# Four steps of the opening moved by one to seven slots: hash of batch 1's first pair, a turn and the load of its second pair, the last value sums of batch 0

## The chip, the cores and the metric

The kernel runs on one core of a Trainium2 chip. The metric is the device time of one launch in microseconds; lower is better. The names of the engines in the profile: PE is TensorE (PEld is its weight load), DVE is VectorE, ACT is ScalarE, POOL is GpSimd, and SP only issues transfers.

## The reference

Attention in which a query sees only keys with the same hash, followed by a gated feed-forward layer over the result. B = 4 batches, H = 8 heads, S = 768 positions, D = 64.

```python
q_bits = (einsum('bhsd,dk->bhsk', q, proj) > 0)          # 6 bits; k_bits likewise
mask = q_bucket[:, :, :, None] == k_bucket[:, :, None, :]
scores = where(mask, scale * q @ k.T, -1e9)
attn = exp(scores - max) ; attn = attn / (sum(attn) + 1e-9)
x = (attn @ v) as 3072 rows of 512
xn = x / sqrt(mean(x * x) + 1e-6) * rms_g
g = xn @ w_gate ; val = xn @ w_val                         # 512 -> 1536
out = (g * sigmoid(g) * val) @ w_out                       # 1536 -> 512
```

All inputs and the output are float32; the kernel multiplies in float16 except for the hash and the turns of q and k.

## The kernel before

**Units and slots.** The work is cut into eight units u, two per batch b, each with half of the batch's 768 queries. For a head of a unit there are three chunks of scores of 256 keys by 384 queries. One chunk is one slot, so there are 8 x 24 slots. Slot t of the main loop (lines 888 to 894) issues `scores` for chunk t + 1 (two matmuls, L349), `probs` for chunk t (one exponential on ACT, L361), and then what the list `plan[t]` holds for the slot, in the order in which it was put there by `at`. The order on every engine and queue is the order of the program: an instruction that waits holds back all that stands behind it on its engine. In its first 16 heads the order goes over the two units of batch 0. The pair-wise numbering (b, hp) means heads 2 hp and 2 hp + 1 of batch b.

**What a pair needs before its scores.** For the four pairs of batch 0 and the first two of batch 1:
- the load: `load_natural` for k and q and `load_v` for v, three transfers of 384 KB on SP's queue (L97, L106), into a ring of eight buffers, tag "L";
- four turns, `turn_pe`: three TensorE transposes each (L156) into a PSUM bank and a copy on DVE to kT or qT (L158);
- casts to float16 in the tile QK (L178, on POOL or DVE);
- the hash, `hash_pair`: sixteen float32 matmuls into two PSUM banks (L238), and two DVE operations that turn their signs into bits (L227);
- `send_pair`: four small transfers on SP's queue (L277) of 6 rows of bits each into rows 64 to 69 of QK, in the order k and q of the first head, k and q of the second. Scores take these six rows along as additional rows of the product, so equal hashes raise the score.

**Sums of the values.** `v_mean` adds the values of a pair over all positions with matmuls against a tile of ones (L333) and scales the result into cvb (L336), a small constant that stands for the 1e-9 in the reference. Batch 0's first pair takes it from one matmul, the other three from six. `attn_out` (L388 to L401) adds cvb to the product of probabilities and values, divides, and squares for the norm; that of the fourth pair runs in slot 31.

**Banks.** All of turns, hashes, sums, gates and projections take their PSUM bank from one ring of three (tag "g", line 60); a step waits until the bank that it takes was read by its last user. Scores have a ring of two of their own, and the products with the values (`av`, L374, two parts per head, in the slots 1 and 2 above a multiple of three) one bank.

**Around the change.** Slots 8 to 17 turn and hash the last pairs of batch 0. Slots 22 to 32 turn and hash the first two pairs of batch 1, whose scores start in slot 47. POOL issues the loads of the gate and value weights in slots 22, 25 and 31 (L585). Slot 31 ends the attention of unit 0; its norm and its transposition follow until slot 37, with a few idle matmuls (L580) in slots 34 to 36. From slot 38 on the matmuls of the feed-forward layer (L484, L513) are spread over the slots.

The times of the steps stand in two tuples. For a pair of batch 1 the second holds: load; four turns (k of both heads, q of both heads; the first is also when the pair's buffers are taken); cast of k; cast of q; hash; send; the value's cast and sums. The hash and the send of the second pair do not go by the tuple but are placed in slots 32 and 38.

Of the kernel before, what the change touches and what calls it, by code (L numbers as in the profile page):

```python
# [33 lines left out]
def kernel(  # L34
# [563 lines left out]
    def at(w, s, f, *a):  # L598
        plan[NS * w + s].append(lambda: f(*a))
# [75 lines left out]
    at(0, 6, v_prep, 0, 1)  # L675
    at(0, 15, v_prep, 0, 2)
    at(0, 19, v_prep, 0, 3, nc.vector)
    for hp, t in enumerate((6, 16, 21, 28)):
        at(0, t, v_mean, 0, hp, 2, *([range(6)] if hp else []))
    for i, (t, t2) in enumerate(((22, 25), (31, 31))):  # L680
        cols = slice(i * DFF // 2, (i + 1) * DFF // 2)
# [2 lines left out]
        at(0, 39 + 3 * i, load_w, wo, moe_w_out, 6 * i, 6)  # L684


    for hp, ts in ((0, (8, 22, 23, 24, 25, 24, 39, 26, 28, 42)), (1, (20, 27, 28, 29, 30, 29, 41, 32, 33, 43))):
        tl, ts = ts[0], ts[1:]
        for w in "kq":
            at(0, tl, load_natural, nc.sync, 1, hp, w)  # L690
        at(0, tl, load_v, nc.sync, 1, hp)
        at(0, ts[0], new_pair, 1, hp)
        for t, hh, w in zip(ts[0:4], (0, 1, 0, 1), "kkqq"):
            at(0, t, turn_pe, 1, hp, hh, w)
        at(0, ts[4], cast_pool, 1, hp, "k")
        at(0, ts[5], cast_pool, 1, hp, "q")
        if hp == 0:
            at(0, ts[6], hash_pair, 1, hp)
            at(0, ts[7], send_pair, 1, hp)
        at(0, ts[8], v_prep, 1, hp)  # L700
        at(0, ts[8], v_sum, 1, hp)
# [33 lines left out]
    for n, (u, h) in enumerate(order):  # L735
        t = 3 * n + 4 - ((u, h) == (0, H - 1))
# [128 lines left out]
    def behind_norm(t):  # L865

        return t - t % NS + 9 if 1 <= t % NS < 9 else t

    for (b, hp), (load, kturns, qturns, _) in spots.items():
# [3 lines left out]
        for w, turns in (("k", kturns), ("q", qturns)):  # L873
            for i, t in enumerate(turns):
                at(0, t, turn_dve, b, hp, w, i, len(turns))
            t = turns[-1] + 1
            at(0, t if (b, hp) == (1, 2) else behind_norm(t), cast_pool, b, hp, w)
        t = 54 if (b, hp) == (1, 2) else behind_norm(qturns[-1] + 2)
# [69 lines left out]
```

## Time and profile before

| | us |
|---|---|
| median of 3 runs (lowest, highest) | 326.93 (326.87, 327.19) |
| the profiled execution | 326.68 |
| its span, first to last instruction | 324.9 |
| PE busy | 319.9 |
| DVE busy | 229.7 |
| ACT busy | 228.4 |
| POOL busy | 157.6 |

The granted clock of TensorE is 0.999 over the span. Rows of the timeline give the start, the length, the engine, the line in the kernel, the operation with its output and inputs, and how often; the bracket at the end is the idle time before and what ended it. Matmuls overlap, so a row's length is longer than the time until the next one starts. Rows of windows give a stretch, its length, the busy time and number of instructions of each engine, the granted clock, the DMA share and the GB/s moved.

### The profile page before, as it was taken

Reading aid. Unit: us, or ns where it says so; the run is one execution under the profiler, and the core shown is the slowest. Engines: PE = TensorE matmul, PEld = TensorE weight load, DVE = VectorE, ACT = ScalarE, POOL = GpSimd, SP = SyncE. Lnnn points to the kernel's source line nnn. Section 1 sums busy time; section 2 is a strip of 40 time slices with the busy share of each in tenths; the row PEclk is TensorE's granted clock in tenths of the full one; section 3 lists DMA queues with packets and bytes.
Section 4 is the critical chain, followed back from the end, with each engine's and each line's share of the span. In section 5 each row is a group of like instructions: output and inputs, shape, how many; then the busy total and the mean of one; then the engine's idle time right before and its main releaser. Section 6 shows DMA issues by size and latency. Waiting matters only on the chain.

```text
span 324.9 us, 7772 instructions
## 1 busy us (share of the span) xinstructions
PE 319.9 (98%) x2955; PEld 194.4 (60%) x2955; DVE 229.7 (71%) x512; ACT 228.4 (70%) x333; POOL 157.6 (49%) x204
## 2 busy tenths in 40 slices
PE   8999999999999999999999999999999999999996
PEld 3676666656566565655566565655666556665554
DVE  5887876859888568874888568785677536673870
ACT  7999887667688676776767776777777768744322
POOL 4999759955974363731883621752582111221000
PEclk9999999999999999999999999999999999999999
DMA  7942999988428864055547056002100030003002
GB/s 208 360 168 85 226 216 195 192 159 151 103 38 158 157 136 88 6 94 156 89 100 145 35 125 120 7 5 66 72 4 3 1 99 34 0 2 105 10 2 97
DMA packets 85741, 32.63 MB, mean 100 GB/s; under 512 B 70908, under 2 KB 82632, under 8 KB 85704
## 3 DMA queue, kind: packets, MB, share of 16 engines
q1 hardware_dynamic: 81800, 27.35, 36.1%
q0 software_dynamic: 3680, 4.72, 8.5%
q8 instruction: 23, 0.38, 0.5%
q14 instruction: 14, 0.11, 0.1%
q10 hardware_dynamic: 224, 0.07, 0.1%
HBM read 28.58 MB, written 6.29 MB: 107 GB/s over the span
## 4 chain that ended last, share of the span: by engine, by line
PE 98%; ACT 1%; DVE 0%; issue 0%
PE s_ps L349 20%; PE g_ps L484 19%; PE v_ps L484 19%; PE y_ps L513 18%; PE o_ps L374 11%; PE d_ps L218 2%; PE t_ps L156 2%; PE d_ps L238 2%; PE z_ps L580 1%; PE x_ps L467 1%; PE y_ps L532 1%; PE m_ps L333 1%; ACT psb L361 1%; DVE kT L158 0%; PE s_ps L156 0%
## 5 line engine op out<-in xcount | busy, mean ns | idle before, releaser
L361 ACT ACTIVATE psb<-s_ps,ebias 128x768 f16<-128x768 f32 x192 | 167.7, 900 | 20.0 <-PE s_ps L349 19.2
L349 PE MATMUL s_ps<-QK 128*128 128x384 f16 (+1 forms) x384 | 93.5, 326 | 1.2 <-ACT psb L361 1.1
L492 ACT ACTIVATE t<-g_ps 128x384 f32<-128x384 f32 x96 | 47.2, 492 | 52.2 <-PE g_ps L484 50.5
L484 PE MATMUL g_ps<-xnT,wg 128*128 128x384 f16 x384 | 82.7, 326 | 0.0
L484 PE MATMUL v_ps<-xnT,wv 128*128 128x384 f16 x384 | 81.8, 326 | 0.0
L501 DVE SCALAR_TENSOR_TENSOR a<-t,g_ps 128x384 f32<-128x384 f32 x96 | 53.0, 552 | 28.9 <-ACT t L492 27.2
L395 POOL TENSOR_TENSOR x<-otmp,rcp 128x384 f32<-128x384 f32 x30 | 25.1, 837 | 96.2 <-DVE rcp L393 95.8
L513 PE MATMUL y_ps<-wo,ht 128*128 128x512 f16 x276 | 67.7, 379 | 0.0
L502 DVE SCALAR_TENSOR_TENSOR ht<-a,v_ps 128x384 f16<-128x384 f32 x96 | 53.2, 554 | 11.5 <-PE v_ps L484 3.6
L374 PEld LDWEIGHTS <-psb 128*128 128x128 f16 x1152 | 51.9, 97 | 15.7 <-issue 1.2
L374 PE MATMUL o_ps<-vl,psb 128*128 128x65 f16 x1152 | 55.8, 193 | 0.0
L349 PEld LDWEIGHTS <-QK 128*128 128x128 f16 (+1 forms) x384 | 34.8, 98 | 33.7 <-issue 7.9
L484 PEld LDWEIGHTS <-wg 128*128 128x128 f16 x384 | 35.2, 97 | 21.2
L484 PEld LDWEIGHTS <-wv 128*128 128x128 f16 x384 | 35.1, 97 | 20.8 <-issue 0.2
L513 PEld LDWEIGHTS <-ht 128*128 128x128 f16 x276 | 24.9, 98 | 23.0
L525 ACT COPY ysb<-y_ps 128x512 f32<-128x512 f32 x23 | 13.5, 587 | 15.8 <-PE y_ps L513 15.8
L388 DVE TENSOR_TENSOR otmp<-o_ps,cvb 128x390 f32<-128x390 f32 x32 | 17.8, 557 | 7.1 <-PE o_ps L374 7.1
L208 POOL CAST QK<-qT 64x768 f16<-64x768 f32 x20 | 16.5, 823 | 10.3 <-DVE qT L195 9.5
L401 POOL TENSOR_TENSOR sq<-x 128x384 f32<-128x384 f32 x24 | 19.9, 828 | 1.9
L208 POOL CAST QK<-kT 64x768 f16<-64x768 f32 x20 | 16.4, 822 | 5.2 <-DVE kT L195 3.1
L473 DVE TENSOR_TENSOR xnT<-x_ps,gcol 128x512 f16<-128x512 f16 x11 | 7.4, 688 | 15.1 <-PE x_ps L467 15.0
L195 DVE STREAM_TRANSPOSE kT<-kL 128x192 f32<-128x192 f32 x32 | 16.4, 516 | 0.0
(85 smaller groups left out, 274.9 us busy)
## 6 DMA issues: line engine op xcount, KB each, us to landing
vn<-in_v_dram SPq DMA_DIRECT2D x16, 384.0 KB
out_dram<-ysb SPq DMA_DIRECT2D x23, 256.0 KB
qL<-in_q_dram SPq DMA_DIRECT2D x40, 96.0 KB
kL<-in_k_dram SPq DMA_DIRECT2D x40, 96.0 KB
kn<-in_k_dram SPq DMA_DIRECT2D x5, 384.0 KB
qn<-in_q_dram SPq DMA_DIRECT2D x5, 384.0 KB
wg<-in_moe_w_gate_dram POOLq DMA_DIRECT2D x2, 768.0 KB, 9.4
wv<-in_moe_w_val_dram POOLq DMA_DIRECT2D x2, 768.0 KB, 11.7
```

The lines of the kernel that those rows point to most:

```text
L208: nc.gpsimd.tensor_copy(QK[b, 2 * hp + hh, "h"][0:64, o : o + S], src[64 * hh : 64 * hh + 64, :])
L349: nc.tensor.matmul(ps[:, j, 0:HALF], QK[b, h, "h"][rows, S + jt * 128 : S + (jt + 1) * 128], QK[b, h, "h"][rows, half * HALF : (half + 1) ...
L361: nc.scalar.activation(psb[u, h][:, 2 * ch : 2 * ch + 2, :], sps.pop((u, i))[:, :, 0:HALF], AF.Exp, bias=ebias, scale=ESCALE,)
L374: nc.tensor.matmul(o[:, c, hh, 0:65], psb[u, h][:, jt, c * 128 : (c + 1) * 128], vls[b % 2][:, h, 2 * (jt % 3) + jt // 3 if b in PARITY el ...
L388: nc.vector.tensor_add(tmp[:, :, :, 0:65], o[:, :, :, 0:65], cvb[b % 2][:, 2 * hp : 2 * hp + 2, 0:65].unsqueeze(1).to_broadcast([128, 3, 2 ...
L395: eng.tensor_mul(xd.rearrange("p c (h d) -> p c h d", h=2), tmp[:, :, :, 0:64], r.to_broadcast([128, 3, 2, 64]),)
L401: eng.tensor_mul(sq, xd, xd)
L484: nc.tensor.matmul(ps, w[:, kt, fs], xnT[u][:, kt, :], start=(kt == 0), stop=(kt == 3))
L492: nc.scalar.activation(t, fbank[u, ft, "g_ps"], AF.Tanh, scale=0.5)
L501: nc.vector.scalar_tensor_tensor(out=a, in0=t, scalar=1.0, in1=g, op0=ALU.add, op1=ALU.mult)
L502: nc.vector.scalar_tensor_tensor(out=ht[u][:, ft, :], in0=a, scalar=0.5, in1=vv, op0=ALU.mult, op1=ALU.mult)
L513: nc.tensor.matmul(y, ht[u][:, ft, c * 128 : (c + 1) * 128], wo[:, ft, :], start=(ft == 0), stop=(ft == NF - 1),)
```

## The change

Four steps are moved to other slots; nothing is added or removed.
- `v_mean` of batch 0's fourth pair goes from slot 28 to slot 21, behind that of the third pair.
- `hash_pair` of (1, 0) goes from slot 26 to slot 27. Its send stays in slot 28.
- The first turn of (1, 1) (k of its first head, with the taking of its buffers) goes from slot 27 to slot 26. The other turns stay.
- The three load transfers of (1, 1) go from slot 20 to slot 17, which on SP's queue is ahead of the four sends of (0, 3) in slot 18.

```diff
-    for hp, t in enumerate((6, 16, 21, 28)):
+    for hp, t in enumerate((6, 16, 21, 21)):
         at(0, t, v_mean, 0, hp, 2, *([range(6)] if hp else []))
...
-    for hp, ts in ((0, (8, 22, 23, 24, 25, 24, 39, 26, 28, 42)), (1, (20, 27, 28, 29, 30, 29, 41, 32, 33, 43))):
+    for hp, ts in ((0, (8, 22, 23, 24, 25, 24, 39, 27, 28, 42)), (1, (17, 26, 28, 29, 30, 29, 41, 32, 33, 43))):
         tl, ts = ts[0], ts[1:]
         for w in "kq":
             at(0, tl, load_natural, nc.sync, 1, hp, w)
         at(0, tl, load_v, nc.sync, 1, hp)
         at(0, ts[0], new_pair, 1, hp)
         for t, hh, w in zip(ts[0:4], (0, 1, 0, 1), "kkqq"):
             at(0, t, turn_pe, 1, hp, hh, w)
```

## The prediction

> **What bounds the kernel now.** I read the page's busy shares and chain first, then the busy time by stage, and then every engine in order of time from 24 to 46 us, where slots 17 to 38 lie. The page:
>
> ```profile
> PE 319.9 (98%) x2955; PEld 194.4 (60%) x2955; DVE 229.7 (71%) x512; ACT 228.4 (70%) x333; POOL 157.6 (49%) x204
> PE 98%; ACT 1%; DVE 0%; issue 0%
> ```
>
> TensorE is the bound over the whole span, and the change removes no matmul. It can only gain where PE stands idle or is held up by something beside it. The busy time by stage (stretch, its length, then PE, PEld, DVE, ACT, POOL, the granted clock, DMA share and GB/s) says where that is:
>
> ```profile
> 25.90:28.43 2.53, 2.11 (x30) 1.51 (x29) 2.04 (x5) 2.53 (x4) 2.34 (x3) 1.00 0.02 7
> 28.43:35.99 7.56, 7.56 (x105) 5.87 (x104) 5.66 (x14) 6.63 (x8) 5.80 (x7) 1.00 0.79 207
> 35.99:44.35 8.36, 8.34 (x120) 5.47 (x118) 7.03 (x21) 8.18 (x13) 4.80 (x6) 1.00 1.21 209
> ```
>
> Slots 19 to 21 (first row): ACT is full, PE idles 0.42 us. Slots 22 to 29 (second row): PE is full, ACT idles 0.93. Slots 30 to 37 (third row): ACT is nearly full, and PE is padded with idle matmuls. PE in order of time:
>
> ```profile
> 26.85 0.48 PE L349 MATMUL s_ps<-QK 70*128 70x384 f16 x2 [0.39 <-ACT psb L361]
> 27.18 0.44 PE L374 MATMUL o_ps<-vl,psb 128*128 128x65 f16 x9
> 27.64 0.48 PE L349 MATMUL s_ps<-QK 70*128 70x384 f16 x2
> 27.97 0.51 PE L333 MATMUL m_ps<-vl,ones 128*128 128x130 f16 x6
> 28.43 0.48 PE L349 MATMUL s_ps<-QK 70*128 70x384 f16 x2
> 28.76 0.49 PE L156 MATMUL t_ps<-ident,kn 128*128 128x128 f32 x3
> ```
>
> The lengths overlap; what an operation costs is the distance to the next start. Scores cost 0.33 (27.64 to 27.97), a turn 0.33, an AV part 0.27 to 0.28, a mean 0.35 (at 23.15 it is followed by AV at 23.50, and at 34.45 by a turn at 34.80). So the mean of slot 21 leaves PE free at 28.32, and the next scores start at 28.43: 0.11 us of slack, the last before PE runs without a gap. The weight loads of the hash in slot 26, and DVE beside them:
>
> ```profile
> 32.30 0.11 PEld L238 LDWEIGHTS d_ps<-kT,pj 64*32 64x32 f32 x2 [0.32 <-issue]
> 32.41 0.14 PEld L238 LDWEIGHTS d_ps<-qT,pj 64*32 64x32 f32 x4
> 33.18 0.33 PEld L374 LDWEIGHTS <-psb 128*128 128x128 f16 x9 [0.62 <-issue]
> 31.15 1.21 DVE L158 COPY qT<-t_ps 128x384 f32<-128x384 f32 x2 [0.37 <-PE t_ps L156]
> ```
>
> The last weights of the hash load at 32.41, just after the DVE copy of the last turn ends (31.15 + 1.21 = 32.36). From the hash's first load to the next operation's it takes 0.88. The hashes of slots 17 and 32, which follow no fresh turn, take 0.80 (24.28 to 25.08, 38.29 to 39.09).
>
> **The change part by part**, on the profiled execution (326.68 us, span 324.9, 1.78 around it).
>
> *Mean of batch 0's fourth pair, slot 28 to 21.* It leaves slot 28, where PE is full: -0.35. In slot 21 it follows the other mean: PE is free at 28.67 instead of 28.32, and the scores that started at 28.43 start at 28.67: +0.24. Its operands are there: DVE wrote that pair's v at 26.18 to 26.73. Its PSUM bank, third in the ring of three, was last read by the signs of slot 17 (over by 26.27). Its DVE scaling (0.27 to 0.29) falls near 28.9, before the turn's copy that starts at 29.29. ACT's chain: its softmax of 29.22 needs scores that now end near 29.20, so it holds; the next two slip by about 0.1 us, which PE does not feel, since it needs each only a slot later.
>
> *Hash of (1,0), 26 to 27; turn of (1,1), 27 to 26.* PE's sum stays, but the hash no longer follows the copy of slot 25 directly: 0.88 becomes 0.80, -0.08. Starts of the scores in slots 26 to 30, before: 31.88, 33.47, 34.12, 35.41, 36.34. After: 32.12, 33.06 (0.33 + 0.33 + 0.28), 34.28 (0.33 + a gap of 0.09 as at 32.21 to 32.30 + 0.80), 35.22, 36.15. ACT gets its scores of slot 27 0.41 earlier and those of slot 28 0.16 later; its 0.63 us gap before 34.00 shrinks and a new one opens before the next softmax. The pair's qT and kT buffers are those of (0,3), whose last cast ended at 28.31. Banks: the hash takes those of the turns of slots 24 and 25, copied by 32.6. The turn of slot 29 now waits for the first sign operation, over near 34.9, and starts at 35.55: 0.6 to spare. The attention output of slot 26 comes ahead of the signs on DVE instead of behind them (34.23 before, about 33.4 after), so POOL, which idled 1.46 us for it, is earlier by the same; no one on the path waits for it. The signs end near 35.4 instead of 34.31, so the four sends of slot 28 leave SP about 1.1 us later and hold back the block loads of slot 34 (37.29 before) by up to that. Those feed DVE turns from 62.02 on, and their last transfer was issued at 56.84: 5 us of cover. If that were gone, DVE's turns of (1,2) would be late next.
>
> *Load of (1,1), 20 to 17.* Three issues on SP (0.39, 0.42, 0.41) now stand ahead of the four sends of (0,3) instead of behind them:
>
> ```profile
> 21.12 2.85 SPq L277 DMA_DIRECT2D QK<-bits  x4
> ...
> 26.30 2.78 SPq L277 DMA_DIRECT2D QK<-bits  x4
> 29.18 0.39 SPq L97 DMA_DIRECT2D kn<-in_k_dram  x1
> ```
>
> SP is free at 23.97 and the bits of (0,3) come only at 26.27, so the issues fit in that hole. The buffers that the loads take (ring of eight) were last read by turns of slots 13 to 16, over by 23.31, so they do not wait, and the sends still issue at 26.30. The data is another matter. The load of (1,0), issued at 17.14, drained until about 21.8; that of (1,1), issued at 24.07, so drains until about 28.7. The first two sends, issued at 26.30 and 27.00, are needed by the scores of slot 23 (29.36 before, 29.60 after). Fine windows show where their data goes now, and where the load and the sends of (0,2) ended:
>
> ```profile
> 21.60:21.80 0.20, 0.20 (x10) 0.20 (x8) 0.20 (x1) 0.20 (x1) 0.20 (x1) 1.00 0.50 177
> 23.20:23.40 0.20, 0.20 (x7) 0.20 (x5) 0.20 (x1) 0.07 (x2) 0.17 (x1) 1.00 0.11 31
> 28.20:28.40 0.20, 0.20 (x5) 0.15 (x3) 0.17 (x2) 0.20 (x2) 0.10 (x1) 1.00 0.11 31
> 28.40:28.60 0.20, 0.20 (x4) 0.10 (x2) 0.12 (x2) 0.20 (x1) 0.02 (x1) 1.00 0.05 15
> ```
>
> The second send now moves its data at 28.2 to 28.6. Behind the load it would at about 28.8. No row shows a send behind a load, so I bound it. Lower end: the second send of (0,2) moved its data at 23.0 to 23.4 and the scores at 23.86 used it without a gap, so 0.5 to 0.8 us from data to use; 28.8 + 0.8 = 29.6, cost 0. Upper end: the 1.3 us from issue to data (26.30 to 27.6) begins only when the load has drained: 28.7 + 1.3 + 0.8 = 30.8, cost 1.2. Below nothing is excluded, since no one waits for these sends now. I take 0: both sends are queued 1.7 us and more before the load ends. The Trainium skill speaks against the change here: DMA: Bandwidth & Descriptors (Queues, rings and completion order) says that a transfer's semaphore write lands only after every earlier write of that DMA engine, across its queues. By that rule the sends cannot land before the load, and the sum stays if they land right behind it; no run shows it yet.
>
> In exchange the load leaves the stretch from 30 to 34 us, in which the gate weights queue behind it. No instruction waits for those weights, so this is worth nothing.
>
> Sum: -0.35 + 0.24 - 0.08 = -0.19 us, or 0.06%. From slot 30 on the same work follows, 0.19 earlier. That gives 326.5 for the profiled execution; the median of the runs shown is 0.25 above it, so 326.7.
>
> **The rivals.**
> - *The sends land late* (slower). The scores of slot 23 wait for the second send; PE, which is full from there on, makes none of it up. Price up to 1.2, so 326.7 + 1.2 = 327.9 at worst, 327.4 in the middle. It decides once the data is usable after 29.8 (loss over the gain of 0.19); for 0.2% slower it must come after 30.45. For: 1.18 MB stands ahead in the same queue. Against: the timing above.
> - *The shift is absorbed* (no change): slots 30 to 37 hang on ACT and on the chain from the attention output through POOL's power (40.62) to the normed x, and if that chain did not move, nothing after it would: 326.9. Against: the chain begins with matmuls that do move, and ACT's gap of 0.30 before 35.99 waits for PE.
> - *ACT sets the pace* (faster): if even slots let ACT run without its gaps of 0.63 and 0.30, it gains 0.93: 326.0. For: ACT is full on both sides of the stretch. Against: PE has no idle time in it to give.
>
> **How the numbers follow.** A measurement of this kernel tells about 0.2% from no change, 0.65 us. The forecast has 0.48 (of it 0.03 beyond 0.65 faster), the absorbed shift 0.14, late sends 0.20 (0.15 beyond 0.65 slower), ACT's pace 0.15 (all faster), some loss that I do not see 0.03. So faster 0.18, same 0.64, slower 0.18. The range goes from 326.1, near the ACT case, to 327.5, past the middle of the late sends.
>
> **What would show it.** In the trace after: two means back to back near 27.97 and the next scores at 28.67; the hash near 33.5, taking 0.80; scores of slot 30 at 36.15; loads on SP near 24.1 and sends at 26.30. Wrong would be an idle PE before the scores near 29.6 (late sends), scores of slot 30 at 35.6 or earlier (ACT's pace), or a first gate matmul that stays at 44.35 (absorbed).

## The result: 0.3% slower, by one wait for a small transfer

The changed kernel takes 328.13 us (median of 6 runs, 327.63 to 328.57); the kernel before took 327.01 beside it. The ratio is 1.003, with a 95% interval of 1.0019 to 1.004: slower, by about 1.1 us. The forecast was 326.7, with a range of 326.1 to 327.5, so the time lies outside it, on the side of the rival "the sends land late".

The profiled execution took 328.11 us, with a span of 326.3. TensorE is still busy for 98% of it, and the page shows hardly more:

```profile
PE 320.6 (98%) x2955; PEld 194.8 (60%) x2955; DVE 229.8 (70%) x512; ACT 228.3 (70%) x333; POOL 157.3 (48%) x204
```

The busy time by stage does. These are two stretches, from the scores of slot 22 to those of slot 30 and from there to the first gate matmul; the first pair of rows is of the kernel before, the second of the changed one:

```profile
28.43:36.34 7.91, 7.91 (x115) 6.21 (x114) 5.85 (x15) 6.98 (x9) 6.08 (x8) 1.00 0.80 207
36.34:44.35 8.01, 7.99 (x114) 5.13 (x111) 6.84 (x20) 7.83 (x13) 4.53 (x6) 1.00 1.21 210
```
```profile
29.17:37.74 8.57, 7.63 (x110) 5.89 (x108) 5.82 (x14) 6.94 (x9) 6.54 (x9) 1.00 0.71 118
37.74:45.75 8.01, 7.99 (x114) 5.13 (x111) 6.85 (x20) 7.83 (x13) 3.93 (x5) 1.00 1.16 196
```

The second stage is the same to 0.01 us. The first is 0.66 longer although PE works 0.28 less in it: PE, full before, now idles 0.94. (With the 0.23 by which the stage starts late, see below, that makes the 0.89 that the change costs.) PE in order of time shows where:

```profile
28.15 0.48 PE L349 MATMUL s_ps<-QK 70*128 70x384 f16 x2
28.47 0.85 PE L333 MATMUL m_ps<-vl,ones 128*128 128x130 f16 x12
29.17 0.49 PE L349 MATMUL s_ps<-QK 70*128 70x384 f16 x2
29.49 0.49 PE L156 MATMUL t_ps<-ident,kn 128*128 128x128 f32 x3
29.82 0.44 PE L374 MATMUL o_ps<-vl,psb 128*128 128x65 f16 x9
31.20 0.48 PE L349 MATMUL s_ps<-QK 70*128 70x384 f16 x2 [0.94 <-DMA QK<-bits]
```

The scores of slot 23 could have started at 30.10 (29.82 + 0.28) and start at 31.20: 1.10 us late, waiting for the hash bits. SP's queue and the chain of waits name the transfer:

```profile
24.58 0.38 SPq L97 DMA_DIRECT2D kn<-in_k_dram  x1
25.06 0.47 SPq L97 DMA_DIRECT2D qn<-in_q_dram  x1
25.63 0.42 SPq L106 DMA_DIRECT2D vn<-in_v_dram  x1
26.80 2.84 SPq L277 DMA_DIRECT2D QK<-bits  x4
...
27.56 3.51 DMA QK<-bits
```

The second send goes out at 27.56 and has landed 3.51 us later; before, it went out at 27.00, landed 1.85 us later, and the scores at 29.36 used it without a gap. (Landings that no row shows are read from the trace's records of completion: a send of 9 KB ends with six marks, and it has landed with the last.)

One thing must be taken off before the two traces can be compared. They differ by 0.51 us at the scores of slot 17 (23.86 before, 24.37 after), ahead of anything that the change touches: in the thirteen profiled executions of this case the first scores start between 6.86 and 7.86 us, and in the trace before they start at 6.86. So all kernels are compared below by the interval from the scores of slot 17 to the first gate matmul. It is 20.49 us before and 21.38 after, +0.89. What follows the gate matmul takes 280.55 us of the span in both. The medians differ by 1.12, which is 0.23 more; the varying start is larger than that, but no trace shows where this rest lies.

### The profile page after: what moved, and what is told of

It reads as the page before. It is cut to its first block, busy times and chain, and to the rows that moved or that the text cites. A ratio compares the mean times of both kernels' runs of the same rounds, so it can differ in the third digit from the quotient of the medians.

```text
span 326.3 us, 7771 instructions
## 1 busy us (share of the span) xinstructions
PE 320.6 (98%) x2955; PEld 194.8 (60%) x2955; DVE 229.8 (70%) x512; ACT 228.3 (70%) x333; POOL 157.3 (48%) x204
## 4 chain that ended last, share of the span: by engine, by line
PE 97%; DMA 1%; DVE 0%; ACT 0%; issue 0%; SPq 0%
PE s_ps L349 19%; PE g_ps L484 19%; PE v_ps L484 19%; PE y_ps L513 18%; PE o_ps L374 10%; PE d_ps L218 2%; PE t_ps L156 2%; PE d_ps L238 2%; PE z_ps L580 1%; DMA QK<-bits 1%; PE x_ps L467 1%; PE y_ps L532 1%; PE m_ps L333 0%; PE s_ps L156 0%; DVE bits L227 0%; ACT psb L361 0%
## 5 line engine op out<-in xcount | busy, mean ns | idle before, releaser
L513 PEld LDWEIGHTS <-ht 128*128 128x128 f16 x276 | 24.8, 97 | 23.0
```

The lines of the kernel that those rows point to most:

```text
L513: nc.tensor.matmul(y, ht[u][:, ft, c * 128 : (c + 1) * 128], wo[:, ft, :], start=(ft == 0), stop=(ft == NF - 1),)
```

## The experiments

Theory A: the load of (1,1), now ahead of the sends of (0,3), makes the second send late, and everything else came as forecast. Theory B: the new order of hash, turn and mean costs the time.

| kernel | interval | against before | median, before beside it | ratio (95%) |
|---|---|---|---|---|
| before | 20.49 | | | |
| the change | 21.38 | +0.89 | 328.13, 327.01 | 1.003 (1.0019 to 1.004) |
| load back in slot 20 | 20.63 | +0.14 | 327.67, 327.30 | 1.0007 (0.9997 to 1.0017) |
| load alone in slot 17 | 21.70 | +1.21 | 328.14, 327.30 | 1.0028 (1.0015 to 1.0041) |
| k alone in slot 17 | 20.28 | -0.21 | 327.06, 327.30 | 0.9992 (0.9981 to 1.0003) |
| k and q in slot 17 | 20.28 | -0.21 | 327.18, 327.30 | 0.9994 (0.9984 to 1.0004) |
| mean alone | 20.42 | -0.07 | 327.55 (one run) | |
| k, k, q as three transfers | 20.99 | +0.50 | 328.01 (one run) | |
| k in slot 17, mean in slot 20 | 20.09 | -0.40 | 326.85, 327.15 | 0.9988 (0.9979 to 0.9998) |
| a fourth transfer in slot 17 | 25.89 | +5.40 | 333.37 (one run) | |
| two more sends, before | 28.22 | +7.73 | 335.68 (one run) | |
| 1.18 MB on ACT's queue, slot 17 | 21.15 | +0.66 | 328.45 (one run) | |
| 1.18 MB on ACT's queue, slot 19 | 26.19 | +5.70 | 333.12 (one run) | |

Each interval is of one profiled execution.

**The parts apart.** The change with the load back in slot 20:

```diff
-(1, (17, 26, 28, 29, 30, 29, 41, 32, 33, 43))
+(1, (20, 26, 28, 29, 30, 29, 41, 32, 33, 43))
```

> The change, but with the load of (1,1) back in slot 20, behind the sends of (0,3). Theory A (the second send of (0,3) waits behind the load, PE idles 1.10 us before the scores of slot 23, everything else came as predicted): the idle time is gone, the scores of slot 24 follow those of slot 23 without a gap, and the time is 0.19 us under the kernel before, or up to 0.3 over it if the turn now in slot 26 has to wait for k of (1,1). Theory B (the reordering of hash, turn and mean costs the time itself, or the start of the run does): 1.1 us over the kernel before, as with the whole change.

The wait is gone, and with it 0.75 of the 0.89. The gain of 0.19 does not show, because two smaller gaps take its place. The turn now in slot 26 starts 0.17 us late, at 33.16: its k, issued at 29.59, landed only at 33.02, so in slot 26 this turn needs an earlier load. The scores of slot 23 start 0.15 us late, at 30.15: the second send landed at 30.01, its last mark 0.76 behind the other five. Such a late mark comes up again below.

The kernel before with only the load moved:

```diff
-(1, (20, 27, 28, 29, 30, 29, 41, 32, 33, 43))
+(1, (17, 27, 28, 29, 30, 29, 41, 32, 33, 43))
```

> The kernel before with only the load moved to slot 17. Theory A: the same late send; the scores of slot 23 are due 0.24 us earlier than with the whole change, so PE idles about 1.3 us there and nothing is gained elsewhere: 1.3 us over the kernel before. Theory B: no difference, within 0.2 us.

```profile
31.06 0.49 PE L349 MATMUL s_ps<-QK 70*128 70x384 f16 x2 [1.05 <-DMA QK<-bits]
```

Those scores were due at 29.85 (28.92 and 0.93 for the slot): 1.21 us late, which is the whole difference of the interval. Theory B falls: the load alone makes the wait, in the old order too.

The mean alone in slot 21:

> The kernel before with only the mean of the fourth pair moved to slot 21. From the scores of slot 17 to the first gate matmul: 0.35 less for slot 28, 0.24 more for slot 21, so 0.11 us less than before (20.38 instead of 20.49). Rival: the later scores of slot 22 cost ACT its chain there, and nothing is gained.

It gains 0.07 instead of 0.11: the turn and the product after it in slot 28 lie 0.38 apart (35.64 to 36.02) instead of 0.33, and the rest is as summed.

**How many bytes.** The load split over the two slots, with k, or k and q, left in slot 17:

```diff
-        for w in "kq":
-            at(0, tl, load_natural, nc.sync, 1, hp, w)
-        at(0, tl, load_v, nc.sync, 1, hp)
+        for w, tw in (("k", 17), ("q", 20)):        # or ("q", 17)
+            at(0, tw if hp else tl, load_natural, nc.sync, 1, hp, w)
+        at(0, 20 if hp else tl, load_v, nc.sync, 1, hp)
```

> The change with only the k transfer of the load in slot 17, q and v in slot 20 (a third of the bytes ahead of the sends). Theory A by bytes: 0.39 MB issued near 24.1 drain by about 26.5, before the sends are issued; no wait, 0.19 us under the kernel before. Rival A2 (any transfer ahead of a send costs it about a microsecond, whatever its size): the wait of about 1.1 us stays, 0.9 over.

> The change with k and q of the load in slot 17 and v in slot 20 (two thirds of the bytes). Theory A by bytes: they drain near 28.1, when the second send would move its data anyway; a wait of 0 to 0.4 us before the scores of slot 23, so 0.2 under to 0.2 over the kernel before. Rival A2: 0.9 over.

Neither waits; both intervals are 0.21 us under the kernel before, where the sum said 0.19 (the medians are too close to show it). In the second, with two thirds of the bytes ahead, slots 22 and 23 take 0.93 each, as they do with a full PE:

```profile
28.69 0.49 PE L349 MATMUL s_ps<-QK 70*128 70x384 f16 x2
29.62 0.49 PE L349 MATMUL s_ps<-QK 70*128 70x384 f16 x2
30.55 0.49 PE L349 MATMUL s_ps<-QK 70*128 70x384 f16 x2
```

The load's data ended near 27.8 here, before the second send's were due, and five of that send's six marks came 1.82 us after its issue (the sixth after 2.33). So rival A2, a fixed cost of about a microsecond behind any transfer, falls. The same two thirds cut into three transfers, k of each head and q:

> The change with three transfers in slot 17 that hold only two thirds of the bytes: k of each head by itself (192 KB each) and q (384 KB); v in slot 20. If bytes decide: no wait before the scores of slot 23 over 0.2 us, as with k and q alone. If the number of transfers ahead decides: the wait of 1.1 us is back.

```profile
29.55 0.44 PE L374 MATMUL o_ps<-vl,psb 128*128 128x65 f16 x9
30.54 0.48 PE L349 MATMUL s_ps<-QK 70*128 70x384 f16 x2 [0.55 <-DMA QK<-bits]
```

0.72 us late (due at 29.82): neither forecast. The load's data ran until 28.5 instead of 27.8 (q went out at 25.34 instead of 24.53, and the rate dipped to 115 GB/s near 27.1), but five of the second send's six marks still came by 29.11, in time. Only the sixth came at 30.40. At 29.02 the trace has one packet of 8 KB on its queue for instructions. In four other runs (load back in slot 20, k alone, mean alone, mean in slot 20) such a packet falls near the sends, with no load in flight, and in each one mark of one send lags the other five by 0.56 to 0.76 us; in the two traces without it (before, two more sends) no mark of a send in quiet queues lags by more than 0.1. So the late mark is probably the instruction packet's and not the load's. No run controls this packet, so that stays an inference.

A fourth transfer behind the three:

```diff
+    def extra_load():
+        nc.sync.dma_start(out=spare_v..., in_=v[1, 2:4]...)      # 384 KB that nothing reads
...
+        if hp:
+            at(0, tl, extra_load)
```

> The change with a fourth transfer of 384 KB behind the three of slot 17, into a buffer that nothing reads, so that a third more bytes stand ahead of the sends. Theory A by bytes: the sends land another 1.0 us later (0.39 MB at the 390 GB/s of the load), so PE idles 2.0 to 2.2 us before the scores of slot 23 instead of 1.10. Rival A2 (a fixed cost of a send behind a load): 1.1 us as before.

```profile
27.93 4.99 DMA QK<-bits
33.06 0.80 PE L356 MATMUL s_ps<-QK 70*128 70x384 f16 x2 [2.53 <-DMA QK<-bits]
33.00:39.40 6.40, 6.34 (x46) 5.09 (x47) 2.18 (x5) 3.32 (x4) 2.33 (x3) 0.52 0.85 132
```

The second send takes 4.99 us instead of 3.51, and the scores (L356 here, the line numbers shift with the added lines), due at 30.37, start 2.69 late: more with more bytes, beyond the 2.0 to 2.2 expected. But the interval grew by 5.40, twice the wait. The third row says why: for 6.4 us after it the granted clock is 0.52, and each matmul takes nearly twice as long.

**In quiet queues, and across queues.** Two further sends ahead of the four, with nothing else in flight, so that PE must wait:

```diff
+                nc.sync.dma_start(out=spare_b[0:6], in_=bt[0:6, :])      # twice, ahead of the sends of (0,3)
```

> The kernel before with two more sends of 9 KB (bits into a buffer that nothing reads) on SP ahead of the four of (0,3), so that each of the four goes out 1.4 us later with nothing else in flight, and PE has to wait for the second. It measures a send's time from issue to use in quiet queues: the scores of slot 23 then start at 28.4 plus that time (in the time of the profile before). With the 1.7 to 2.4 us that the prediction assumed they start at 30.1 to 30.8, an idle PE of 0.8 to 1.4 us. If they start later, the send itself is slower than assumed, and less of the 3.5 us with the load ahead is due to the load.

```profile
27.17 1.88 DMA spare_b<-bits
...
31.90 5.75 DMA QK<-bits
```

A send alone takes 1.88 us from issue to landing: the second of the two extra sends waits for the first and says so directly, and the delayed scores agree (issue at 30.49, start at 32.47). The expected 1.7 to 2.4 held for quiet queues. The other row is more telling: the fourth send went out at 31.90, with a weight load on POOL's queue just issued (31.13) and the load of (1,1) behind it in its own queue (32.66), and took 5.75. From 32.8 to 36.8 the trace counts 381 packets of the weights' queue and none of SP's: the send's own data waited, and the load behind it had moved nothing yet, so it was the weights on the other queue that held the send. PE's first wait of 2.23 us was again followed by half the clock: 0.50 from 33.6 to 43.6. PE was busy for 8.70 us of that, so the clock cost about 4.4 us (an estimate, half of 8.70); the waits for the second and the fourth send are the rest of the 7.73 by which this interval is longer.

Last, 1.18 MB on ACT's queue instead of SP's, in the kernel before:

```diff
+    def extra_load(eng):
+        eng.dma_start(out=wo..., in_=v[1, 0:6]...)      # into wo, which is loaded later
...
+            at(0, 17, extra_load, nc.scalar)            # 19 in the second run
```

> The kernel before with an additional transfer of 1.18 MB in slot 17 on ACT's queue instead of SP's (values of batch 1 into the space of the output weights, which is overwritten later), the load of (1,1) still in slot 20. If the order within SP's own queue holds the sends: no wait before the scores of slot 23 beyond 0.3 us. If the DMA engines or the completion of a send hold them whatever queue the bytes are on: PE idles there for 0.5 to 1.3 us, less than 1.3 by what ACT's issue delays PE before that.

```profile
23.89 0.41 ACTq L91 DMA_DIRECT2D wo<-in_v_dram  x1
28.01 0.48 PE L357 MATMUL s_ps<-QK 70*128 70x384 f16 x2 [1.11 <-DMA QK<-bits]
```

The wait came three slots early, at the scores of slot 20: the last send of (0,2), issued near 23.7, met the transfer, although that was issued 0.15 us behind it. From 24.8 to 26.8 the trace counts 253 packets of ACT's queue and none of SP's, and the send landed at 27.87, 4.1 us after its issue. ACT would have allowed these scores at 27.29 (0.39 idle, as in the other runs), so 0.72 of the wait is the send's. PE then reached slot 23 too late to test the sends of (0,3). So the transfer was put out in slot 19:

> As the run with 1.18 MB on ACT's queue, but the transfer goes out in slot 19, after the sends of (0,2) have landed, so that only the sends of (0,3) can meet it, and PE reaches the scores of slot 23 on time. If the order within SP's queue holds a send: no wait there over 0.3 us. If any bytes in flight on the DMA engines hold its completion: the transfer drains from about 27 to 30.6 and PE waits 0.5 to 2.0 us before the scores of slot 23 for bits whose sends were issued at about the same time as the transfer.

```profile
26.13 0.41 ACTq L91 DMA_DIRECT2D wo<-in_v_dram  x1
27.23 5.48 DMA QK<-bits
32.84 0.80 PE L357 MATMUL s_ps<-QK 70*128 70x384 f16 x2 [3.09 <-DMA QK<-bits]
31.40:38.20 6.80, 5.36 (x35) 4.00 (x35) 1.94 (x4) 2.70 (x3) 2.42 (x4) 0.50 1.11 269
```

Nothing stood ahead of the sends on SP's queue, and the second took 5.48 us. So the order in SP's queue is not needed to hold them; a transfer in flight on another queue is enough. What waits is the sends' data: from 27.0 to 30.6 the trace counts 670 packets of ACT's queue and none of SP's. The prediction cited a rule from the Trainium skill, DMA: Bandwidth & Descriptors (Queues, rings and completion order), that a semaphore write waits for all earlier writes of its DMA engine, across queues. The late landings agree with it, but the waiting data are more than it says, and no run here separates the two.

**A version that is faster.** Only k in slot 17, and the mean of the fourth pair in slot 20:

```diff
-    for hp, t in enumerate((6, 16, 21, 21)):
+    for hp, t in enumerate((6, 16, 21, 20)):
```

> The change with only k of the load in slot 17 (q and v in 20) and the mean of the fourth pair in slot 20 instead of 21. Slot 20 has 0.18 us of idle PE behind its products and slot 21 0.11 behind its mean, so the two means cost 0.06 instead of 0.24 more than one: by the sum of the prediction 0.35 - 0.06 + 0.08 = 0.37 us under the kernel before, where the change without the late send had 0.19. Rival: ACT is full there, and its chain slips by what PE gains; then 0.2 under, as without the step.

```profile
27.42 0.48 PE L349 MATMUL s_ps<-QK 70*128 70x384 f16 x2 [0.39 <-ACT psb L361]
27.75 0.51 PE L333 MATMUL m_ps<-vl,ones 128*128 128x130 f16 x6
28.37 0.49 PE L349 MATMUL s_ps<-QK 70*128 70x384 f16 x2
28.70 0.51 PE L333 MATMUL m_ps<-vl,ones 128*128 128x130 f16 x6
29.04 0.49 PE L349 MATMUL s_ps<-QK 70*128 70x384 f16 x2
```

From the first of these scores to the last it takes 1.62 us, against 1.58 before with one mean (26.85 to 28.43): the second mean is almost free. The interval is 0.40 us shorter (0.37 expected), and the time 0.9988 of the kernel before, with an interval of 0.9979 to 0.9998. It beats the changed kernel clearly and the kernel before by little: the upper end of that interval is barely under 1.

## Why the prediction was wrong, point by point

- *Means in slot 21, +0.24, and out of slot 28, -0.35*: right. The scores of slot 22 come 0.23 later than before when the start is taken off (29.17 - 28.43 - 0.51).
- *Hash without a fresh turn ahead, -0.08*: right. It starts at 35.06 and the scores behind it at 35.87, 0.81. From the scores of slot 23 to those of slot 30 it takes 6.54 us instead of 6.98: -0.44, where -0.43 was summed.
- *Banks, buffers, DVE, SP's later loads cost nothing*: nothing shows there; the stage behind slot 30 is the same.
- *The load's issues fit in SP's hole*: right, 24.58 to 26.05, and the sends went out at 26.80 as soon as the bits were there.
- *The sends behind the load, "I take 0"*: this step failed. The term measured 1.10 us, near the upper end of 1.2 that was kept for the range. The step took it that the second send moves its data right behind the load, so that the scores can use it by 29.6; they used it at 31.20, which is 30.69 in the time of the trace before. The reason given for the lower end was that the sends are queued 1.7 us before the load ends; that does not help, since the second lands, at 31.06, about 1.3 us after the load's data ends:

```profile
28.80:29.00 0.20, 0.20 (x8) 0.20 (x6) 0.14 (x1) 0.20 (x2) 0.01 (x1) 1.00 0.96 361
29.60:29.80 0.20, 0.20 (x4) 0.20 (x3) 0.06 (x1) 0.19 (x2) 0.20 (x1) 1.00 0.29 95
30.20:30.40 0.20, 0.06 (x2) 0.00 (x0) 0.20 (x1) 0.20 (x1) 0.20 (x1) 1.00 0.13 31
```

  In these windows of the changed kernel (GB/s last) the load runs at full rate until 29.2 and is gone by 29.8; what follows is the size of the last sends. The end of the load's data was forecast rightly (28.7 is 29.2 here). The lower end was also built from a send that met a finished load, the one row that could not tell.

  How the 1.10 divides is in part open: an instruction packet falls at 29.67 in this execution too, and the send's sixth mark came 0.70 us behind the fifth. The load alone in slot 17, with no such packet near the sends, waited 1.21.

  "No row shows a send behind a load" missed a case. The trace before held four sends behind a large transfer of another queue: those of (1,0), from 34.34 on, with the gate weights in flight. Nobody waits for them, so no wait gives them away, but from 34.8 to 38.2 that trace counts 398 packets of the weights' queue and none of SP's, and these sends landed 4.9 to 5.3 us after their issue.

With that term the sum is -0.19 + 1.10 = +0.91, and the interval shows +0.89. So the mechanism of the rival "the sends land late" is what happened, with the chance of 0.20 that it was given; "the shift is absorbed" and "ACT sets the pace" did not occur.

## What to carry to other kernels

A small transfer that an engine waits for can be held by a large one in flight, on its own queue or another, issued ahead of it or, in one run here, 0.15 us behind. Here 1.85 us became 3.5 with 1.18 MB ahead on the same queue, 5.0 with 1.57, and 5.5 with 1.18 MB on another. A trace can show this before anyone waits for it: count the packets of each queue while a small transfer should move. When a load is moved earlier, look which small sends it will then overlap and how much slack their readers have; moving only what is needed first, a third of the bytes here, kept the gain of 0.2 in the interval. And where two costs of an unknown term lie far apart, a row in which the two transfers did not meet says nothing for the lower one.

## What was not expected of the hardware

- A large transfer on one queue stopped another queue altogether: with sends of SP waiting, SP's queue moved no packet from 27.0 to 30.6 beside ACT's (slot 19; the sends went out from 26.52 on) and from 32.8 to 36.8 beside the weights' (two more sends).
- PE's idle time can cost twice. After 1.10 and 1.21 us of waiting the granted clock stayed at 1.00; with 2.23, 2.69 and 3.25 it fell to about 0.5 for 7 to 10 us, and the intervals grew by 5.4 to 7.7 us. It did not fall at the end of the wait: with 2.69 and 3.25 about 2.0 and 1.7 us after the scores were due, while PE still stood idle, with 2.23 about 1.1 us after PE had resumed. The Trainium skill, TensorE: Matmul & The Clock Gate (HAM oscillation — how this bites in real kernels), says that gaps above about 3.4 us are to be avoided; here 2.23 was enough. So a price of late sends that is worked out at full clock, as the range's upper end was, holds for the shorter waits alone.
- The start of a launch varies by up to 1.0 us between executions (first scores at 6.86 to 7.86), about as much as the whole change costs. Intervals inside the trace told the parts apart where medians could not.
